# Attention and soft mixture of experts on one core: where v's factor is computed, when the next batch's inputs are loaded and split, and the order of the opening

## The chip, the core and the metric

The kernel runs on one core of one Trainium2 chip. The metric is the device time of one execution in microseconds (us). The core's engines run side by side and each works through its own list in order: TensorE (PE in the profile, with its weight loads as PEld) multiplies matrices into PSUM; VectorE (DVE) and ScalarE (ACT) do the element-wise work; GpSimd (POOL) does almost nothing here; SyncE (SP) issues the transfers (DMA) between HBM and the on-chip memory SBUF, also one after the other. An instruction that waits for another engine holds up everything behind it on its own list.

## The reference

```python
B, S, D, d_qk = 8, 2496, 256, 64
scores = (z @ z.T) / S                       # per batch, 2496 x 2496, symmetric
out    = u * (np.maximum(scores, 0) ** 2 @ v)
x      = out.reshape(8 * 2496, 256)
logits = x @ phi                             # 19968 x 32
d = softmax of logits over the tokens;  slots = d.T @ x
slot_out = relu(slots @ w1[e]) @ w2[e]       # 8 experts, 4 slots each
c = softmax of logits over the 32 slots;  result = c @ slot_out
```

The attention with relu and square takes most of the time: per batch, 2496 x 2496 scores and their product with v. Everything is single precision outside. Inside, z, the squared scores and v are each split into two half-precision parts (high and low), and three of the four products are summed. The half-precision parts need factors that bring the data into range: one per block of z, and one for v that depends on the largest bound over all of v in the batch.

## The kernel before, in words

**Tiling.** A batch has 5 blocks of 512 tokens (the last is padded to 448). For every block of queries (a *chunk*) the kernel runs through the 5 blocks of keys in two *halves* of 256 keys each, so a batch is 50 halves; with the last batch, whose last block is worked in two chunks of 256 queries, there are 410. The main loop `for h, x in enumerate(halves)` has one *step* per half. Step h puts the sums of half h on PE (`sums_halves` or `sums_whole`: 12 products of 128 rows and 512 columns, or 24 of 64 rows), and prepares a later half (`prepare(k)`, from step 18 on k = h + 3): PE computes the scores into the one PSUM tile `sc`, ACT applies relu and square into `r`, ACT or DVE rounds to half precision (`ph`), DVE subtracts to get the low part (`pl`). There are four buffers each of `r`, `ph` and `pl`, so at most some three halves can be ready ahead of PE.

**Symmetry.** A block pair that was computed once is not computed again: DVE transposes `r` (`y`), SP stores it to a scratch in HBM (`turned`), and later chunks fetch it back (`r<-turned`). Those halves are called turned: they need no scores, no relu and no square. In a batch's first chunk all ten halves are computed, in its last chunk (halves 40 to 49) eight of ten are turned. `lent` and `rd` are the same for the pair of a block with itself.

**Running sums.** A chunk's result gathers in a PSUM tile `acc`. There are two of these, used in turn; `next_acc()` takes the next one. When a chunk is finished, DVE multiplies it with u and `out_by` into `xg` (`finish_chunk`).

**The next batch's inputs.** While batch b-1 runs, z and v of batch b are brought in. The dictionary `splits` says at which step `load_z` or `load_v` is called (SP issues the load two steps before the number written there), and at which steps the functions that it returns run. These are, for z, `bound` (DVE, largest square) and `split` (ACT high part, DVE low part); for v, `squares` (ACT, tile `vq`, sum of squares into `energy`), `high` (ACT) and `low` (DVE). Raw data lands in 12 buffers with the tag `raw`, which z (5 tiles) and v (10 tiles) share: the eighth v load needs the buffer of the first z tile, and so on. The split parts go to 16 `blk` buffers for 15 tiles a batch.

**Factors.** `add_bounds` (a product with ones on PE) and `factors` (DVE) give z's. For v's, `largest` (DVE) leaves one number per partition in `few`; `scale_v(b, ps)` has PE spread these numbers over the PSUM tile `ps` in four small products, DVE reduces them back into `few` and computes `v_by` and `out_by`. `later` says at which steps these run. Before the change both `add_bounds` and `scale_v` take their PSUM tile with `next_acc()`, so that tile is afterwards the `acc` of the next chunk. `scale_v` is called at step 39 of the old batch, the last of its fourth chunk, and so uses the tile in which the fifth chunk's sums begin at step 40.

**Order.** Every PE, ACT, DVE and SP instruction goes through the class `InOrder` (line 74), which keeps the written order on each engine; that is why nearly all rows of the profile have the line L74, and tiles are the way to tell them apart. Small work is queued in the lists `middle`, `turning` and `behind` and run inside `prepare`: `behind` comes after the half's own work. `landing` and `later` feed `behind`.

**The token groups.** When 1024 tokens of x are complete, `groups(q)` adds fourteen small items to `work`, one per step. One of them computes the logits in the PSUM tile `ms`, of which there is one; the same tile also receives the slot sums of the group before. In the profile both have the name `lg`.

**Opening.** Before the loop, batch 0's z and v are loaded. z is bounded and scaled block by block (`first_z`, `add_bounds`, `factors`, `raise_z`), v's squares (`measure_v`), `largest` and `scale_v` follow, `keep_busy(n)` puts 2n products of ones on PE, and `prepare` is called for halves 0 to 3. One v tile is split before the loop and one in each step (`split_first_v`).

Of the kernel before, what the change touches and what calls it, by code (L numbers as in the profile page):

```python
# [8 lines left out]
F32 = mybir.dt.float32  # L9
# [4 lines left out]
AF = mybir.ActivationFunctionType  # L14
# [4 lines left out]
P = 128  # L19
# [6 lines left out]
QC = 512  # L26
# [5 lines left out]
NP = KT // 4  # L32
# [4 lines left out]
CATCH = 18  # L37
# [40 lines left out]
def attn_soft_moe_kernel(ctx, tc, uT, v, zz, phi, ww, outT):  # L78
    nc = tc.nc

    pe, act, dve, sp = (InOrder(tc, x) for x in (nc.tensor, nc.scalar, nc.vector, nc.sync))
# [73 lines left out]
    def add_bounds(b, ps, js):  # L155
        pe.matmul(
            ps[:, 0, js], nc.const_aps.tensor(1.0, [P, P], F32), tops[b % 2][:, js], start=True, stop=True
        )

    def factors(b, ps, js):  # L160


        n2, by = (t[b % 2][:, js] for t in (norm2, z_by))
        dve.tensor_scalar(bits(n2), bits(ps[:, 0, js]), EVEN, None, op0=ALU.bitwise_and)
        dve.tensor_scalar(
            bits(by), bits(n2), EVEN, 1, op0=ALU.bitwise_xor, op1=ALU.logical_shift_right
        )
        dve.tensor_scalar_mul(by, by, 2.0**77)
# [21 lines left out]
    def largest(b):  # L190


        root, w = v_by[b % 2], few[b % 2]
        n2 = norm2[b % 2].unsqueeze(2).to_broadcast([P, NP, 2])
        dve.tensor_scalar(
            bits(root), bits(energy[b % 2]), 1, ROOT, op0=ALU.logical_shift_right, op1=ALU.bitwise_and
        )
        r2 = root.rearrange("p (j i) -> p j i", i=2)
        dve.tensor_mul(r2, r2, n2)
        dve.reduce_max(w[:, 0:1], root, axis=AX.X)  # L200

    def scale_v(b, ps):


        w = few[b % 2]
        ps = ps[:, :, 2 * PAD :]
        for h, rows in enumerate(HALF):
            pe.matmul(
                ps[:, h], w[rows, 0:1].to_broadcast([64, P]), ident[rows, rows],
                start=True, stop=True,  # L210
            )
        dve.tensor_reduce(w[:, 2:4], ps, axis=AX.X, op=ALU.max)
        dve.scalar_tensor_tensor(w[:, 1:2], w[:, 2:3], 2.0**-120, w[:, 3:4], op0=ALU.max, op1=ALU.max)
        dve.tensor_scalar(
            bits(w[:, 2:3]), bits(w[:, 1:2]), EXPONENT, EXPONENT, op0=ALU.bitwise_and, op1=ALU.bitwise_xor
        )
        n2 = norm2[b % 2].unsqueeze(2).to_broadcast([P, NP, 2])
        dve.tensor_scalar(
            v_by[b % 2].rearrange("p (j i) -> p j i", i=2), n2, w[:, 2:3], 2.0**-51, op0=ALU.mult, op1=ALU.mult
        )  # L220
        dve.tensor_scalar(
            out_by[b % 2], norm2[b % 2], w[:, 1:2], 2.0**40 / S**2, op0=ALU.mult, op1=ALU.mult
        )
# [82 lines left out]
    halves = []  # L306
# [42 lines left out]
    def scores(k, ps=None, cut=slice(None)):  # L349


        x = halves[k]
        b, p = x.b, x.p
        j, o, n, t0 = x.ch
        if ps is None:
            ps = sc_ps.tile([P, 2, QC], F32, tag="sc", name=f"sc_{k}")
        m_all = QC if x.padded else n
        m = m_all // 2 if x.borrows else m_all

        def keys(t, c):  # L360
            return t[:, c * P : (c + 1) * P]

        i0 = 2 * x.borrows

        def queries(t):
            t = t.rearrange("k (i a q) -> k a i q", i=4, q=NS)
            return t[:, o // P : (o + m_all) // P, i0:][:, cut]

        def out(h):
            return ps[:, h, :m].rearrange("p (a i q) -> p a i q", i=4 - i0, q=NS)[:, cut]  # L370

        if k < RAW_SCORES:
            for h, rows in enumerate(HALF):
                pe.matmul(
                    out(h), keys(zraw[b, p][rows], 2 * x.w + h), queries(zraw[b, j][rows]),
                    start=True, stop=True,
                )
        else:
            zk, zq = zt[b, p], zt[b, j]
            for i, (kl, ql) in enumerate(((0, 0), (0, 1), (1, 0))):  # L380
                for h, rows in enumerate(HALF):
                    pe.matmul(
                        out(h), keys(zk[rows, kl], 2 * x.w + h), queries(zq[rows, ql]),
                        start=(i == 0), stop=(i == 2),
                    )
        return ps, m
# [3 lines left out]
    def high_low(k):  # L390

        if halves[k].ch[2] >= PAD + PAD:
            return [wa.tile([P, 2, QC], F16, tag=t, name=f"{t}_{k}", bufs=4) for t in ("ph", "pl")]
        i, j = divmod(k % 4, 2)
        if i not in quarters:
            quarters[i] = [
                wa.tile([P, 2, 2, QC // 2], F16, tag=t, name=f"{t}_{k}", bufs=4) for t in ("ph", "pl")
            ]
        return [t[:, j] for t in quarters[i]]

    def prepare(k):

# [451 lines left out]
    splits, later = {}, {}  # L854
    for b in range(1, B):
        base, order = (b - 1) * 2 * NP * NQ, BLOCKS[b == B - 1]
        z_at = [31, 32, 33, 39, 41]
        v_at = [47, 42, 43, 44, 45, 46, 48, 49, 50, 51]
        for i, (j, at) in enumerate(zip(order, z_at)):
            splits.setdefault(base + 11 + 2 * i, []).append((load_z, b, j, [base + 14 + 2 * i, base + at]))  # L860
        for i, at in enumerate(v_at):
            splits.setdefault(base + 27 + i, []).append(
                (load_v, b, i, [base + 27 + i, base + at, base + at])
            )
        later[base + 37] = lambda b=b: largest(b)
        later[base + 39] = lambda b=b: scale_v(b, next_acc())
        later[base + 25] = lambda b=b: add_bounds(b, next_acc(), slice(0, NP))
        later[base + 26] = lambda b=b: factors(b, accs[-1], slice(0, NP))
    landing, fetched = {}, set()
    accs = []  # L870

    def next_acc():

        accs.append(acc_ps.tile([P, 2, QC], F32, tag="acc", name=f"acc_{len(accs)}"))
        return accs[-1]
# [26 lines left out]
    def split_first_v():  # L902
        if v_splits:
            for f in v_splits.pop(0):
                f()
# [18 lines left out]
    def keep_busy(n):  # L924
        for _ in range(n):
            for h, rows in enumerate(HALF):
                pe.matmul(idle[:, h], ones[rows, 0:P], ones[rows], start=True, stop=True)
# [7 lines left out]
    def raise_z(p):  # L935
        dve.tensor_scalar_mul(zraw[0, p], zraw[0, p], z_by[0][:, p : p + 1])

    def measure_v(n):
        for _ in range(n):
            first_v.pop(0)()  # L940

    for js in (slice(0, 1), slice(1, 2), slice(2, NP)):
        for p in range(*js.indices(NP)):
            first_z[p]()
        add_bounds(0, idle, js)
        factors(0, idle, js)
        if js.start < 2:
            raise_z(js.start)
            keep_busy(2)
    prepare(0)  # L950
    measure_v(2)
    prepare(1)
    measure_v(8)
    keep_busy(8)
    for p in range(2, NP):
        raise_z(p)
    largest(0)
    scale_v(0, idle)
    prepare(2)
    split_first_v()  # L960
    prepare(3)
    acc = None
    for h, x in enumerate(halves):
        if x.begins:
            chunk = h // (2 * NP)
            acc = accs[chunk] if chunk < len(accs) else next_acc()
        last = len(halves) - h
        transfers(h)
        weights(last)
        if work and (x.at > 1 or last <= 20):  # L970
            work.pop(0)()
        behind.extend(landing.pop(h, ()))
        ahead = [k for k in range(h + 2 + (h > CATCH), h + 3 + (h >= CATCH)) if k < len(halves) and k >= 4]
        split_first_v()
        if not ahead and h < 2:
            run(middle)
            run(turning)
            run(behind)
            sums_halves(h, acc, 1, sums_halves(h, acc, 0, None))
        elif ahead and not halves[ahead[0]].turned:  # L980
            turn = sums_halves(h, acc, 0, None)
            prepare(ahead.pop(0))
            sums_halves(h, acc, 1, turn)
        else:
            if ahead and not x.ends:
                prepare(ahead.pop(0))
            elif not ahead:
                run(middle)
                run(behind)
                between_last(3 - last)  # L990
            sums_whole(h, acc)
        if x.ends:
            finish_chunk(x.b, x.ch, acc)
        for k in ahead:
            prepare(k)
        if h in FIRST_Z:
            z_splits.pop(FIRST_Z[h])()
        del pend[h]
# [300 lines left out]
```

## Time and profile before

| | us |
|---|---|
| median of 3 runs | 1387.83 (1386.79 to 1391.26) |
| the profiled execution's own time | 1392.14 |
| its span, first to last instruction | 1390.4 |
| PE busy in the span | 1283.8 |
| DVE busy | 1101.2 |
| ACT busy | 936.1 |
| one batch, about | 160 |
| first product with v on PE | at 31.66 |

PE's busy time counts a product at its modelled length, and products overlap, so 92% busy doesn't mean 92% of the peak. PE's clock is granted in steps, and a product takes twice as long at 0.50. The times of the table are of one execution; rows of a timeline carry the start, the length, the engine, the operation, output and inputs, and in brackets how long the engine stood idle before it and who released it.

### The profile page before, as it was taken

How to read it: one execution, taken by the hardware profiler on the slowest of the kernel's cores; microseconds unless marked ns; L12 is line 12 of the kernel's file. 1: busy time of each engine (PE TensorE's matmuls, PEld its weight loads, DVE VectorE, ACT ScalarE, POOL GpSimd, SP SyncE). 2: the span in 40 equal slices, each digit the busy share in tenths (PEclk: the TensorE clock that was granted, in tenths of full speed). 3: DMA queues.
4: the chain of work that ended last, by engine and by line, in shares of the span. 5: the costliest groups of instructions: out<-in, count | busy, mean ns of one | idle time of the engine just before them, and what ended most of it. 6: DMA issues, size and time to landing. Idle time of an engine off the chain costs nothing.

```text
span 1390.4 us, 27647 instructions
## 1 busy us (share of the span) xinstructions
PE 1283.8 (92%) x10969; PEld 617.5 (44%) x10969; DVE 1101.2 (79%) x1587; ACT 936.1 (67%) x1220; POOL 3.7 (0%) x22
## 2 busy tenths in 40 slices
PE   5999899998999799997999989998999989989984
PEld 2344355444544344443554444443554444434752
DVE  4788789777997779786998679877898679867663
ACT  5676788575966678575886658667886668754453
POOL 0000000000000000000000000000000000000000
PEclk7999999999999999999999999999999999999995
DMA  3577828784687737877387756878287766979959
GB/s 129 135 216 237 271 60 214 236 272 157 153 255 235 247 98 186 260 252 227 92 246 222 268 147 154 269 240 276 61 229 239 251 194 166 265 223 292 334 210 382
DMA packets 136402, 298.88 MB, mean 215 GB/s; under 512 B 17872, under 2 KB 38864, under 8 KB 124240
## 3 DMA queue, kind: packets, MB, share of 16 engines
q1 hardware_dynamic: 136272, 297.11, 69.9%
q8 instruction: 86, 1.41, 0.4%
q14 instruction: 44, 0.36, 0.1%
HBM read 162.04 MB, written 113.77 MB: 198 GB/s over the span
## 4 chain that ended last, share of the span: by engine, by line
PE 52%; DMA 14%; ACT 12%; DVE 9%; SPq 6%; issue 5%; DVEq 0%; ACTq 0%; POOLq 0%
PE acc L74 40%; PE sc L74 7%; SPq L74 6%; ACT r L74 6%; DMA r<-turned 4%; DMA vr<-in_v 4%; ACT ph L74 3%; DVE pl L74 3%; DVE y L74 2%; PE lg L74 2%; DMA turned<-y 2%; PE pf L74 1%; DMA w_own<-in_w 1%; ACT vq L74 1%; DMA xt<-y 1%
## 5 line engine op out<-in xcount | busy, mean ns | idle before, releaser
L74 PE MATMUL acc<-ph,v 64*128 64x512 f16 (+5 forms) x5036 | 944.5, 372 | 34.1 <-DVE few L74 30.1
L74 PEld LDWEIGHTS <-v 64*128 64x128 f16 (+1 forms) x7554 | 477.3, 96 | 569.3 <-issue 89.2
L74 PE MATMUL acc<-pl,v 64*128 64x512 f16 (+5 forms) x2518 | 608.7, 371 | 2.2 <-DVE pl L74 1.7
L74 DVE TENSOR_TENSOR pl<-r,ph 128x1024 f16<-128x1024 f32 (+1 forms) x410 | 467.3, 1146 | 166.2 <-ACT ph L74 154.7
L74 ACT CAST ph<-r 128x1024 f16<-128x1024 f32 (+1 forms) x286 | 288.3, 1017 | 149.2 <-PE acc L74 85.7
L74 ACT ACTIVATE r<-sc 128x1024 f32<-128x1024 f32 (+1 forms) x242 | 229.0, 946 | 144.7 <-PE sc L74 140.8
L74 ACT ACTIVATE r<-r 128x1024 f32<-128x1024 f32 (+1 forms) x242 | 238.4, 985 | 6.9
L74 DVE STREAM_TRANSPOSE y<-r 128x1024 f32<-128x1024 f32 x160 | 197.9, 1237 | 0.0
L74 PE MATMUL sc<-z,z 64*128 64x512 f16 x912 | 124.7, 377 | 7.6 <-ACT r L74 7.3
L74 PEld LDWEIGHTS <-z 64*128 64x128 f16 x1380 | 71.0, 94 | 90.0 <-issue 23.5
L74 ACT ACTIVATE vq<-vr 128x512 bf16<-128x512 f32 x80 | 49.8, 623 | 64.0 <-DMA vr<-in_v 63.7
L74 DVE CAST ph<-r 128x1024 f16<-128x1024 f32 (+1 forms) x124 | 74.1, 598 | 22.2 <-ACT r L74 21.8
L74 DVE SCALAR_TENSOR_TENSOR xg<-acc,out_by,ut 128x1024 f32<-128x1024 f32 (+7 forms) x57 | 51.5, 925 | 10.4 <-PE acc L74 10.4
L74 DVE SCALAR_TENSOR_TENSOR v<-vr,v_by,v 128x512 f16<-128x512 f32 x80 | 57.9, 724 | 0.0
L74 ACT ACTIVATE v<-vr,v_by 128x512 f16<-128x512 f32 x80 | 57.0, 715 | 0.0
L74 PE MATMUL sc<-z 64*128 64x512 f16 (+1 forms) x468 | 50.8, 321 | 5.1 <-ACT r L74 5.1
L74 DVE STREAM_TRANSPOSE y<-xg 128x512 f32<-128x512 f32 x72 | 49.4, 686 | 0.0
L74 DVE TENSOR_TENSOR pl<-rd,ph 128x512 f16<-128x512 f32 x36 | 23.9, 662 | 21.7 <-ACT ph L74 21.7
L74 DVE COPY ot<-pf 128x1024 f32<-128x1024 f32 (+1 forms) x20 | 24.0, 1198 | 21.0 <-PE pf L74 20.1
L74 ACT COPY ot<-pf 128x1024 f32<-128x1024 f32 (+1 forms) x20 | 19.8, 991 | 24.9 <-PE pf L74 20.7
L74 PE MATMUL lg<-xt 64*32 64x256 f32 x576 | 24.8, 402 | 12.1 <-DMA xt<-y 6.6
L74 ACT CAST ph<-rd 128x512 f16<-128x512 f32 x36 | 21.8, 605 | 11.6 <-DMA rd<-lent 11.6
(184 smaller groups left out, 540.7 us busy)
## 6 DMA issues: line engine op xcount, KB each, us to landing
turned<-y SPq DMA_DIRECT2D x320, 256.0 KB, 4.8
r<-turned SPq DMA_DIRECT2D x76, 1024.0 KB, 6.3
xt<-y SPq DMA_DIRECT2D x288, 72.0 KB, 3.1
vr<-in_v SPq DMA_DIRECT2D x80, 256.0 KB, 5.5
outT<-ot SPq DMA_DIRECT2D x18, 1024.0 KB, 6.9
ut<-in_uT SPq DMA_DIRECT2D x31, 512.0 KB, 5.6
lent<-yd SPq DMA_DIRECT2D x144, 64.0 KB, 2.9
rd<-lent SPq DMA_DIRECT2D x36, 256.0 KB, 3.7
```

What stands on the lines that cost most here:

```text
L74: return lambda *a, **k: self.tc.keep_in_program_order(f(*a, **k))
```

## The change

There are three edits.

1. **v's factor.** `scale_v(b, ...)` at step 39 takes an `ms` tile of its own instead of `next_acc()`. The fifth chunk's `acc` is then taken at step 40 by the loop. `largest` moves from step 37 to 36.
2. **Loads and splits of the next batch.** z's loads and bounds come two steps earlier. z's splits move from steps 31, 32, 33, 39, 41 to 27, 28, 29, 30, 39. v's load numbers go from 27 ... 36 to 23 ... 29 and 32, 33, 34, and `squares` runs one step after that number instead of at it: three steps after the load is issued instead of two, at steps 24 to 30 and 33 to 35. `add_bounds` and `factors` move from 25 and 26 to 23 and 24. The splits of v stay.
3. **Opening.** The new `prepare_first(k)` issues scores and relu and returns square, high and low as three functions. z's first block alone is measured and raised, half 0's scores and relu follow at once, then all ten squares of v on ACT; z's other blocks are measured after that. Half 0 is squared on DVE, not on ACT. `largest` and `scale_v` stand before the last steps of half 1, two v tiles are split before the loop, and half 3 is prepared inside the loop at step 1.

```diff
+    def prepare_first(k):
+        r = wa.tile([P, 2, QC], F32, tag="r", name=f"r_{k}", bufs=4)
+        pend[k] = hi, lo = high_low(k)
+        ps, _ = scores(k)
+        act.activation(r, ps, AF.Relu, scale=2.0**-22)
+        def square():
+            if k:
+                act.activation(r, r, AF.Square)
+            else:
+                dve.tensor_mul(r, r, r)
+        def high():
+            dve.tensor_copy(hi, r)
+        def low():
+            dve.tensor_sub(lo, r, hi)
+        return square, high, low
...
-        z_at = [31, 32, 33, 39, 41]
+        z_at = [27, 28, 29, 30, 39]
+        v_from = [23, 24, 25, 26, 27, 28, 29, 32, 33, 34]
         v_at = [47, 42, 43, 44, 45, 46, 48, 49, 50, 51]
         for i, (j, at) in enumerate(zip(order, z_at)):
-            splits.setdefault(base + 11 + 2 * i, []).append((load_z, b, j, [base + 14 + 2 * i, base + at]))
-        for i, at in enumerate(v_at):
-            splits.setdefault(base + 27 + i, []).append(
-                (load_v, b, i, [base + 27 + i, base + at, base + at])
+            splits.setdefault(base + 9 + 2 * i, []).append((load_z, b, j, [base + 12 + 2 * i, base + at]))
+        for i, (start, at) in enumerate(zip(v_from, v_at)):
+            splits.setdefault(base + start, []).append(
+                (load_v, b, i, [base + start + 1, base + at, base + at])
             )
-        later[base + 37] = lambda b=b: largest(b)
-        later[base + 39] = lambda b=b: scale_v(b, next_acc())
-        later[base + 25] = lambda b=b: add_bounds(b, next_acc(), slice(0, NP))
-        later[base + 26] = lambda b=b: factors(b, accs[-1], slice(0, NP))
+        later[base + 23] = lambda b=b: add_bounds(b, next_acc(), slice(0, NP))
+        later[base + 24] = lambda b=b: factors(b, accs[-1], slice(0, NP))
+        later[base + 36] = lambda b=b: largest(b)
+        later[base + 39] = lambda b=b: scale_v(b, ms_ps.tile([P, 2, 512], F32, tag="ms", name=f"mx_{b}"))
...
-    for js in (slice(0, 1), slice(1, 2), slice(2, NP)):
+    def measure_z(js):
         for p in range(*js.indices(NP)):
             first_z[p]()
         add_bounds(0, idle, js)
         factors(0, idle, js)
-        if js.start < 2:
-            raise_z(js.start)
-            keep_busy(2)
-    prepare(0)
-    measure_v(2)
-    prepare(1)
-    measure_v(8)
-    keep_busy(8)
+    measure_z(slice(0, 1))
+    raise_z(0)
+    keep_busy(1)
+    first = prepare_first(0)
+    measure_v(2 * NP)
+    measure_z(slice(1, 2))
+    raise_z(1)
+    for f in first:
+        f()
+    keep_busy(3)
+    measure_z(slice(2, NP))
+    keep_busy(3)
+    second = prepare_first(1)
+    second[0]()
+    keep_busy(3)
+    largest(0)
+    scale_v(0, idle)
+    second[1]()
+    split_first_v()
+    second[2]()
+    split_first_v()
     for p in range(2, NP):
         raise_z(p)
-    largest(0)
-    scale_v(0, idle)
     prepare(2)
-    split_first_v()
-    prepare(3)
...
-        ahead = [k for k in range(h + 2 + (h > CATCH), h + 3 + (h >= CATCH)) if k < len(halves) and k >= 4]
+        ahead = [k for k in range(h + 2 + (h > CATCH), h + 3 + (h >= CATCH)) if k < len(halves) and k >= 3]
         split_first_v()
-        if not ahead and h < 2:
+        if not ahead and h < 1:
```

## The prediction

> **What bounds the kernel now.** I read the page's first part, then who TensorE (PE) waits for, then the timeline around the longest of those waits.
>
> ```profile
> PE 1283.8 (92%) x10969; PEld 617.5 (44%) x10969; DVE 1101.2 (79%) x1587; ACT 936.1 (67%) x1220; POOL 3.7 (0%) x22
> ```
> ```profile
> PE acc L74 <- DVE few L74: 38.3, 14, 4.4
> ```
> PE has the least room, and its largest wait is for DVE's `few`: 14 waits, two at each of the seven changes of batch. The first of the seven, in the timeline of all engines:
>
> ```profile
> 161.27 1.23 DVE L74 TENSOR_TENSOR pl<-r,ph 128x1024 f16<-128x1024 f32 x1
> 161.38 0.44 PE L74 MATMUL acc<-ident,few 64*128 64x64 f32 x4 [0.35 <-DVE few L74]
> ...
> 163.94 1.21 DVE L74 TENSOR_TENSOR pl<-r,ph 128x1024 f16<-128x1024 f32 x1
> 165.06 0.74 DVE L74 SCALAR_TENSOR_TENSOR z<-zr,z_by,z 128x512 f16<-128x512 f32 x1
> 165.73 0.28 DVE L74 TENSOR_REDUCE few<-acc 128x2 f32<-128x128 f32 x1
> ...
> 166.06 0.91 PE L74 MATMUL acc<-ph,v 128*128 128x448 f16 x2 [4.25 <-DVE few L74]
> ...
> 166.70 1.22 DVE L74 TENSOR_TENSOR pl<-r,ph 128x1024 f16<-128x1024 f32 x1
> ```
> PE writes v's four small products into the next `acc` and cannot start half 40 in that tile until DVE has read them. DVE reads them only at 165.73, behind work for later halves, the old chunk's result and z's last split. The wait also costs clock. Windows, columns PE, PEld, DVE, ACT, POOL busy, then the granted clock: one inside the wait, then the 6 us after the first and the last of the seven restarts:
>
> ```profile
> 164.00:165.00 1.00, 0.00 (x0) 0.00 (x0) 1.00 (x2) 0.00 (x0) 0.00 (x0) 0.50 0.47 90
> ```
> ```profile
> 166.06:172.06 6.00, 6.00 (x20) 2.61 (x20) 2.40 (x6) 1.67 (x2) 0.00 (x0) 0.62 1.02 396
> ...
> 1126.93:1132.93 6.00, 6.00 (x25) 2.80 (x25) 3.03 (x7) 1.73 (x3) 0.00 (x0) 0.76 0.65 206
> ```
> At 0.50 a product takes twice its time, so what is lost is (1 - clock) x 6 us. With the seven clocks 0.62, 0.76, 0.61, 0.60, 0.69, 0.76, 0.76 that is 2.28 + 1.44 + 2.34 + 2.40 + 1.86 + 1.44 + 1.44 = 13.2 us. Waits and clock together are 38.3 + 13.2 = 51.5 us, or 7.36 us per change of batch.
>
> **Edit 1, v's factor.** With `ms` as the target, half 40 no longer waits for DVE's reduction. The four products (0.44 us) and DVE's five small operations stay. The work order decides whether PE then merely waits for the next thing. A half of this chunk takes PE 2.27 us, by the chain of waits:
>
> ```profile
> 185.65 2.27 PE acc L74 x24
> ```
> From 161.82 it needs the low parts `pl` of halves 40, 41, 42, 43 at 161.8, 164.1, 166.3 and 168.6. By the timeline the `pl` that starts at 161.27 is half 41's (ready 162.5), that of 163.94 half 42's (165.15), that of 166.70 half 43's (167.92). All are in time, the last by 0.7 us.
>
> Later DVE has to keep up: PE's chunk shrinks by 7.36 us and DVE's work doesn't. Windows from the wait to the moment at which half 49 is ready, and over the new batch's first chunk, and the two rows of half 49:
>
> ```profile
> 161.82:189.25 27.43, 23.19 (x194) 11.47 (x196) 20.42 (x36) 12.01 (x19) 0.00 (x0) 0.88 0.35 122
> ...
> 194.81:227.00 32.19, 31.87 (x298) 16.70 (x296) 31.14 (x38) 29.74 (x34) 0.00 (x0) 1.00 0.72 173
> ```
> ```profile
> 188.56 0.69 DVE L74 TENSOR_TENSOR pl<-r,ph 128x512 f16<-128x512 f32 x1
> ...
> 192.46 0.54 PE L74 MATMUL acc<-ph,v 64*128 64x448 f16 x4
> ```
> Half 49 is ready at 189.25, 3.2 us before PE takes it. Afterwards PE takes it at 192.46 - 7.36 = 185.1, and DVE, without any gap, has it at 161.82 + 20.42 - 0.74 (z's low part, moved ahead by edit 2) = 181.5. DVE can't be quite gapless, since each rounding waits for a buffer that PE frees, so the lead shrinks by up to some 1.5 us, and in the first chunk DVE is busy 31.14 of 32.19 us and can't rebuild it. I take all 1.5 as lost: 7.36 - 1.5 = 5.86 us per change, **41.0 us** for seven. Bounds: 51.5 (nothing lost), and 23.5 (the first rival below).
>
> Does the clock's share come back too? It does if no long wait remains. [...]
>
> **Edit 2, loads and splits.** ACT waits for v's raw data, and SP is held by z's late splits, because the eighth to tenth v load reuses z's buffers:
>
> ```profile
> ACT vq L74 <- DMA vr<-in_v: 63.7, 21, 6.3
> ```
> ```profile
> SPq L74 <- DVE z L74: 28.4, 15, 3.9
> ```
> ```profile
> vr<-in_v SPq DMA_DIRECT2D x80, 256.0 KB, 5.5
> ```
> ```profile
> 200.82 2.59 PE acc L74 x24
> 204.06 2.59 PE acc L74 x24
> ```
> A load lands 5.5 us after issue, and the square stands two steps behind it. PE's sums of a half take 2.59 us, with scores between them the pitch is 204.06 - 200.82 = 3.24. Two steps are 2 x 2.59 = 5.2 us, too short. Three steps are 7.8 us. Three of ten squares per batch wait now. What it costs PE shows in the windows ahead of two of the changes, where ACT catches up:
>
> ```profile
> 300.00:312.00 12.00, 10.72 (x101) 5.18 (x99) 8.93 (x11) 11.87 (x21) 0.00 (x0) 1.00 0.76 253
> 786.00:798.00 12.00, 9.61 (x86) 4.56 (x83) 9.71 (x14) 11.84 (x21) 0.00 (x0) 1.00 0.66 236
> ```
> PE lacks 1.28 us in the first and 2.39 us in the second, 1.84 on average. Against it: squares now also stand at steps 24 and 25, where ACT prepares direct halves with relu, square and cast:
>
> ```profile
> L74 ACT CAST ph<-r 128x1024 f16<-128x1024 f32 (+1 forms) x286 | 288.3, 1017 | 149.2 <-PE acc L74 85.7
> L74 ACT ACTIVATE r<-sc 128x1024 f32<-128x1024 f32 (+1 forms) x242 | 229.0, 946 | 144.7 <-PE sc L74 140.8
> L74 ACT ACTIVATE r<-r 128x1024 f32<-128x1024 f32 (+1 forms) x242 | 238.4, 985 | 6.9
> ...
> L74 ACT ACTIVATE vq<-vr 128x512 bf16<-128x512 f32 x80 | 49.8, 623 | 64.0 <-DMA vr<-in_v 63.7
> ```
> ```profile
> 159.97 0.72 ACT L74 ACTIVATE z<-zr,z_by 128x512 f16<-128x512 f32 x1
> ```
> That is 0.95 + 0.99 + 1.02 + 0.62 + 0.19 (the read of the sum behind each square, as in the opening's row at 24.31) = 3.77 us of ACT against PE's pitch of 3.24 us: 0.5 us behind in two steps, 1.1 us per batch, covered by the halves prepared ahead; without that cover 7 x 1.1 = 7.7 us lost. The z splits in steps 28 to 30 fall on turned halves, where ACT has 1.02 + 0.72 + 0.81 = 2.55 us in PE's 2.59. The z loads two steps earlier and `add_bounds` at 23 only need data and an `acc` that are ready by then; I cost them at nothing, under PE's sums. I take half of what PE lacks, 0.9 x 7 = **6.3 us**; bounds -7.7 and 1.83 x 7 = 12.8.
>
> **Edit 3, opening.** Rows of the timeline:
>
> ```profile
> 5.52 0.49 DVE L74 TENSOR_SCALAR cw<-cw,z_by 128x512 f32<-128x512 f32 x1
> ...
> 11.00 2.08 PE L74 MATMUL sc<-cw 64*128 64x512 f32 x4
> ...
> 13.13 1.02 ACT L74 ACTIVATE r<-sc 128x1024 f32<-128x1024 f32 x1 [10.90 <-PE sc L74]
> ...
> 24.31 0.19 ACT L74 ACTIVATION_READ_ACCUMULATOR vq<-vr 128x1 f32 x1
> ...
> 26.69 0.22 DVE L74 TENSOR_SCALAR v_by<-norm,few 128x10 f32<-128x10 f32 x1
> ...
> 27.79 1.02 ACT L74 ACTIVATE r<-sc 128x1024 f32<-128x1024 f32 x1 [3.30 <-PE sc L74]
> ...
> 31.66 0.61 PE L74 MATMUL acc<-ph,v 64*128 64x512 f16 x2 [0.71 <-ACT v L74]
> ```
> Block 0 of z is raised at 6.0 in both. After the change its scores follow at once (to 8.3) and relu (to 9.4), then ten squares at 0.62 + 0.19 less overlap, 0.75 us each: to 17.0, if v has landed by then. DVE has the other z blocks and half 0's square, cast and low part (some 3.1 us at 1.2, 0.7, 1.2): to about 15.5. Then PE: ones (I put 1.0, half of the scores' time), half 1's scores (2.08), ones again (1.0), the factor's products (0.44): 20.0. `v_by` then comes at about 21, not 26.9. v's first split is now ahead of half 2's preparation, so PE's first sums start after half 2's scores, at 22 to 23 instead of 31.66, about 9 us earlier. Half 3 is prepared only inside the loop and takes back 1 to 2 us. I take **7.5 us**. Upper bound: ACT starts 13.13 - 8.3 = 4.8 us earlier, loses its pause of 3.3 us between 24.5 and 27.8 and one square (0.99): 9.1. Lower: the 4.8 less a pause of 1.6 until half 1's scores: 3.
>
> **Sum.** 41.0 + 6.3 + 7.5 = 54.8 us off the profiled execution's own 1392.14 (its span of 1390.4 and 1.7 around it) gives 1337.3. That execution lies 4.3 us above the median, 1387.83, so the median should come to **1333**. With all lower bounds (23.5 - 7.7 + 3 = 18.8) it is 1369, with all upper ones (51.5 + 12.8 + 9.1 = 73.4) 1314.
>
> **Rivals.**
> *DVE takes PE's place.* If no lead is left when the new batch begins, its first six steps, in which v's splits go on, run at DVE's pace. By the low parts' starts of 194.75 and 198.44 a half takes 3.7 us there, and I put DVE's need at 3.9 at most, PE's is 3.24: 6 x 0.66 = 4.0 us per change given back, 3.36 x 7 = 23.5 us stay, and the median is 1387.8 - 23.5 - 6.3 - 7.5 = 1350. For it: DVE's 31.14 of 32.19. Against: half 49's 3.2 us of lead.
>
> ```profile
> 194.75 1.23 DVE L74 TENSOR_TENSOR pl<-r,ph 128x1024 f16<-128x1024 f32 x1
> ...
> 198.44 1.23 DVE L74 TENSOR_TENSOR pl<-r,ph 128x1024 f16<-128x1024 f32 x1 [0.35 <-ACT ph L74]
> ```
> *The wait moves to the logits.* `ms` has one buffer, and in four of the seven changes the logits come right behind half 41:
>
> ```profile
> 173.01 1.89 PE lg L74 x64
> ...
> 972.56 1.89 PE lg L74 x64
> ```
> These are the first and the last of the four. PE would get there at 161.82 + 2 x 2.27 = 166.4, DVE's reduction ends at 166.01: 0.4 us in hand. If DVE is late by more, those four changes keep their wait and their clock: 4 x 5.86 = 23.4 us, median 1356.
> *No gain.* DVE and ACT set the pace everywhere and PE's waits only move: 1388. Against: the rows behind the restarts, where DVE is busy 2.40 and 3.03 us of 6 and so not at its limit.
> *Slower.* The squares now stand among the fetches of turned halves. If SP issues a load more than 7.8 - 5.5 = 2.3 us late, its square waits again, and ACT's list is in order: relu and casts of the next halves stand behind it. With all ten squares of a batch waiting the present mean of 63.7 / 21 = 3.0 us, ACT loses 30 us per batch instead of 9.1. The cover is three halves, 7.8 us; the rest, 30 - 9.1 - 7.8 = 13 us, falls on PE: 7 x 13 = 92 us lost against 41.0 + 7.5 gained, 1431. It decides from about eight waiting squares a batch on ((48.5 / 7 + 9.1 + 7.8) / 3.0). Against: only three of ten wait with two steps.
>
> **How the numbers follow.** Forecast (1316 to 1345) 0.58; DVE in PE's place 0.18; logits 0.11; still faster than 1316, 0.03; no gain 0.04; slower 0.06. A difference under 0.3%, 4 us, can't be told from none. Faster: 0.58 + 0.18 + 0.11 + 0.03 = 0.90, same 0.04, slower 0.06. The range of 1314 to 1369 holds the forecast and the first two rivals, 0.87, and both sums of the bounds.
>
> **What would show it.** Edit 1: no wait of PE for `few` above 1 us, clock 1.00 around the changes of batch, DVE near 0.9 behind them. Edit 2: fewer than seven waits of ACT for `vr` in all, and PE without gaps in the 20 us ahead of a change. Edit 3: the first `acc` product at 22 to 23, and half 3's some 8 us earlier than before. The forecast is wrong if a new wait of over 2 us stands at the changes (for `pl`: the first rival; for `lg`: the second), or if ACT's waits for `vr` grow (the last).

## The result, and the profile after

The median fell from 1389.55 to 1308.85 us (1306.67 to 1309.35; the kernel before ran beside it, 1386.79 to 1394.17). The ratio is 0.9413, with a 95% interval of 0.9383 to 0.9443: 80.7 us off. The forecast was 1333 in a range of 1314 to 1369. The direction was right and the size too small, by more than all upper bounds together allowed (73.4 us). The profiled execution took 1308.94 us, its span is 1307.1.

The first part of the page of the kernel after with the shares of its chain, and the chain's shares before:

```profile
PE 1257.1 (96%) x10965; PEld 608.6 (47%) x10965; DVE 1100.1 (84%) x1588; ACT 934.2 (71%) x1219; POOL 3.7 (0%) x22
...
PE 74%; DMA 9%; ACT 8%; DVE 4%; SPq 3%; issue 2%; ACTq 0%; DVEq 0%; POOLq 0%
```
```profile
PE 52%; DMA 14%; ACT 12%; DVE 9%; SPq 6%; issue 5%; DVEq 0%; ACTq 0%; POOLq 0%
```

DVE's and ACT's busy times are those of before. PE's fell by 26.7 us with the same products but for four of ones: 7.0 us of it in the opening and 15.9 in the six batches between the changes, where the mean clock rose from 0.98 to 1.00 (windows below). Its idle time within the span fell from 1390.4 - 1283.8 = 106.6 to 1307.1 - 1257.1 = 50.0. PE's share of the chain that ended last rose from 52% to 74%.

Where the 83.3 us of span went is read from four windows of each trace. They end at half 4's scores in the opening, at the first and at the seventh of v's small products (one set at each change of batch), and at the end of the span. The columns are the window, its length, PE, PEld, DVE, ACT and POOL busy, the clock, and the DMA share and rate. Before:

```profile
0.00:41.90 41.90, 26.75 (x122) 9.63 (x124) 20.27 (x46) 20.09 (x35) 2.93 (x20) 0.80 0.39 124
41.90:161.38 119.48, 116.19 (x891) 50.91 (x887) 96.14 (x121) 93.16 (x117) 0.00 (x0) 1.00 0.72 215
...
161.38:1122.25 960.87, 908.67 (x7657) 430.27 (x7657) 799.89 (x1153) 675.92 (x870) 0.00 (x0) 0.98 0.70 207
...
1122.25:1390.40 268.15, 232.21 (x2303) 126.64 (x2303) 184.94 (x269) 146.91 (x200) 0.79 (x2) 0.91 0.77 258
```

After:

```profile
0.00:28.62 28.62, 19.75 (x118) 8.42 (x120) 18.55 (x45) 19.55 (x35) 2.93 (x20) 0.82 0.45 157
28.62:144.83 116.21, 114.93 (x891) 51.65 (x887) 99.03 (x124) 92.86 (x118) 0.00 (x0) 1.00 0.77 228
...
144.83:1046.18 901.35, 892.81 (x7657) 423.60 (x7656) 797.96 (x1153) 674.56 (x870) 0.00 (x0) 1.00 0.74 220
...
1046.18:1307.10 260.92, 229.64 (x2304) 124.96 (x2303) 184.57 (x269) 147.27 (x199) 0.79 (x2) 0.92 0.80 265
```

The opening gave 13.3 us, the rest of batch 0 3.3, the six batches between the changes 59.5 and the last change with its tail 7.2. In the six batches PE's busy time fell by 908.67 - 892.81 = 15.9 us and its idle time from 52.2 to 8.5, so by 43.7. The waits of PE between the first and the last change say which idle time. Before, and then after (total us, times, longest):

```profile
PE acc L74 <- DVE few L74: 33.7, 12, 4.4
PE sc L74 <- ACT r L74: 10.8, 22, 1.7
```
```profile
PE lg L74 <- DMA xt<-y: 5.8, 7, 2.2
PE sc L74 <- ACT r L74: 1.7, 6, 0.3
```

The wait for `few` is gone as a wait of PE, and the wait of the scores for ACT's `r` has shrunk by 9.1 us. The two make 42.8 of the 43.7. The first of them was in the forecast as a row; the second was not looked at as a term of its own.

At the first change of batch, the timeline after shows:

```profile
144.83 0.44 PE L74 MATMUL mx<-ident,few 64*128 64x64 f32 x4
...
149.34 0.28 DVE L74 TENSOR_REDUCE few<-mx 128x2 f32<-128x128 f32 x1
...
149.84 1.09 PE L74 MATMUL lg<-xg,phi_sb 64*32 64x256 f32 x32
```

DVE's reduction is as far behind the small products as before (4.5 us, before 161.38 to 165.73 = 4.35), but PE has sums to work on. It reaches the logits 0.2 us after the reduction ends. Behind this change the clock is full, and DVE close to its limit:

```profile
150.00:156.00 6.00, 6.00 (x87) 3.25 (x76) 5.83 (x15) 3.27 (x7) 0.00 (x0) 1.00 1.03 397
```

On ACT and SP, the waits that edit 2 was about, after:

```profile
ACT vq L74 <- DMA vr<-in_v: 11.6, 9, 2.5
```
```profile
SPq L74 <- DVE z L74: 1.7, 3, 0.8
```

The squares' wait fell from 63.7 to 11.6 us, SP's wait for z's splits from 28.4 to 1.7.

### The profile page after: what moved, and what is told of

The parts are those of the page before. It is cut to its first block, busy times and chain, and to the rows that moved or that the text cites. A ratio compares the mean times of both kernels' runs of the same rounds, so it can differ in the third digit from the quotient of the medians.

```text
span 1307.1 us, 27632 instructions
## 1 busy us (share of the span) xinstructions
PE 1257.1 (96%) x10965; PEld 608.6 (47%) x10965; DVE 1100.1 (84%) x1588; ACT 934.2 (71%) x1219; POOL 3.7 (0%) x22
## 4 chain that ended last, share of the span: by engine, by line
PE 74%; DMA 9%; ACT 8%; DVE 4%; SPq 3%; issue 2%; ACTq 0%; DVEq 0%; POOLq 0%
PE acc L74 59%; PE sc L74 9%; ACT r L74 4%; SPq L74 3%; PE lg L74 3%; DMA xt<-y 2%; DMA r<-turned 1%; DVE pl L74 1%; DMA w_own<-in_w 1%; ACT ph L74 1%; DMA outT<-ot 1%; PE pf L74 1%; DMA turned<-y 1%; DVE y L74 1%; ACT v L74 1%
## 5 line engine op out<-in xcount | busy, mean ns | idle before, releaser
L74 PE MATMUL acc<-ph,v 64*128 64x512 f16 (+5 forms) x5036 | 930.9, 369 | 1.7 <-DVE ph L74 0.6
L74 PEld LDWEIGHTS <-v 64*128 64x128 f16 (+1 forms) x7554 | 470.3, 95 | 525.5 <-issue 40.2
L74 PE MATMUL acc<-pl,v 64*128 64x512 f16 (+5 forms) x2518 | 602.3, 369 | 1.5 <-DVE pl L74 1.2
L74 DVE CAST ph<-r 128x1024 f16<-128x1024 f32 (+1 forms) x124 | 74.1, 598 | 10.5 <-ACT r L74 10.2
L74 ACT ACTIVATE vq<-vr 128x512 bf16<-128x512 f32 x80 | 49.8, 623 | 11.8 <-DMA vr<-in_v 11.6
L74 PE MATMUL lg<-xt 64*32 64x256 f32 x576 | 24.7, 405 | 11.6 <-DMA xt<-y 6.2
L74 DVE TENSOR_TENSOR pl<-rd,ph 128x512 f16<-128x512 f32 x36 | 23.9, 664 | 11.8 <-ACT ph L74 11.8
```

Of the source, the lines that this page charges most:

```text
L74: return lambda *a, **k: self.tc.keep_in_program_order(f(*a, **k))
```

## The experiments

Each kernel ran in three rounds beside the kernel before (medians of before 1390.26, 1390.34 and 1392.0 us in the three groups). The ratios can be compared with each other and with the 0.9413 of the whole change.

| | median us | ratio to before (95%) |
|---|---|---|
| edit 1 alone | 1347.31 | 0.9679 (0.9646 to 0.9712) |
| edit 2 alone | 1369.78 | 0.9847 (0.9820 to 0.9873) |
| edit 3 alone | 1378.14 | 0.9907 (0.9876 to 0.9938) |
| edits 2 and 3 | 1353.24 | 0.9727 (0.9703 to 0.9751) |
| after, squares two steps behind the issue | 1308.46 | 0.9424 (0.9403 to 0.9446) |
| after, z's splits late again | 1308.05 | 0.9413 (0.9386 to 0.9441) |
| after, all of z late again | 1308.06 | 0.9403 (0.9374 to 0.9432) |
| after, `largest` at step 37 | 1308.39 | 0.9422 (0.9398 to 0.9446) |
| after, v's loads and squares late again | 1326.80 | 0.9541 (0.9499 to 0.9583) |
| after, opening without ones | 1305.88 | 0.9404 (0.9373 to 0.9435) |
| after, one more low part at each change | 1313.51 | 0.9443 (0.9410 to 0.9475) |
| after, three more | 1340.16 | 0.9638 (0.9598 to 0.9678) |

### Which edit gives how much

**Edit 1 alone**, on the kernel before:

```diff
-        later[base + 39] = lambda b=b: scale_v(b, next_acc())
+        later[base + 39] = lambda b=b: scale_v(b, ms_ps.tile([P, 2, 512], F32, tag="ms", name=f"mx_{b}"))
```

> The kernel before with edit 1 alone: v's factor in the logits' tile; largest, loads, splits and opening as before. Theory A (the whole loss of waits and clock at the seven changes of batch comes back, with no help from the other edits): 51.5 us off, about 1338 where before is 1389.5, and no wait of PE for few above 1 us. Theory B (the prediction: DVE's lead shrinks): 41 us off, about 1348. Theory C (DVE has no lead without the earlier loads, and PE waits for pl or for largest instead): 30 us or less off, 1360 or more, with PE still waiting 1 to 3 us for few ahead of the small products.

It took 43.0 us off (1390.26 - 1347.31). PE's waits in the whole run:

```profile
PE mx L74 <- DVE few L74: 7.9, 7, 1.7
```

The second wait of each change is gone. The first is still there under another tile's name: the small products themselves wait for `few`, which `largest` leaves late. So this edit could never have had the whole row of 38.3 us. Its own share is 38.3 - 7.9 = 30.4 us of waits and 13.2 of clock, 43.6 together, and it got nearly all of that.

**Edit 2 alone** is the loop's dictionary of after with `scale_v` in `next_acc()`:

```diff
-        z_at = [31, 32, 33, 39, 41]
+        z_at = [27, 28, 29, 30, 39]
+        v_from = [23, 24, 25, 26, 27, 28, 29, 32, 33, 34]
...
-                (load_v, b, i, [base + 27 + i, base + at, base + at])
+                (load_v, b, i, [base + start + 1, base + at, base + at])
```

> The kernel before with edit 2 alone: loads, bounds, squares, z's splits, add_bounds and largest at the new steps; v's factor still in the next acc, opening as before. Theory A (edit 2 saves PE about 2.6 us per batch by itself): 18 us off, about 1371. Theory B (the prediction's size, 0.9 us per batch): 6 us off, 1383. Theory C (the long wait at the change lets DVE and ACT catch up, so that earlier loads are worth little while it stands): 0 to 4 us off, 1386 to 1390, though ACT's waits for vr fall from 63.7 to about 12 us.

It took 20.5 us off, three times the forecast's 6.3. PE's waits in the whole run:

```profile
PE acc L74 <- DVE few L74: 32.7, 7, 4.9
...
PE sc L74 <- ACT r L74: 4.8, 10, 1.1
```

Seven waits for `few` are left of fourteen. The first of each pair has gone with this edit, and 9.9 us of the scores' waits for `r` with it (14.7 before).

**Edit 3 alone** is the kernel after with the loop's dictionary of before. **Edits 2 and 3** are the kernel after with one line back:

```diff
-        later[base + 39] = lambda b=b: scale_v(b, ms_ps.tile([P, 2, 512], F32, tag="ms", name=f"mx_{b}"))
+        later[base + 39] = lambda b=b: scale_v(b, next_acc())
```

> The kernel after with the whole block of later steps (edits 1 and 2) put back as before, so edit 3 alone. Theory A (read from the two traces, where the scores of half 4 start at 28.62 instead of 41.90): 13.3 us off, 1376. Theory B (the prediction): 7.5 us off, 1382. Nothing in the batches behind should change: the seven waits for few stay at 38 us.

> The kernel after with v's factor back in the next acc: edits 2 and 3. If the edits add up, the time is that of before less what e2 and e3 save; against the kernel after it is longer by what e1 saves: 1309 + 51.5 = 1360 (theory A) or 1309 + 41 = 1350 (theory B). If edit 2 only helps together with edit 1, it is 1374 to 1376, the opening's gain alone.

Edit 3 alone took 12.1 us off, edits 2 and 3 together 37.0. The three edits alone add up to 43.0 + 20.5 + 12.1 = 75.6 us, and together they gave 80.7. The intervals of the single ratios are some 4 us wide to each side, so a joint gain of 5 us is not shown. On top of the other two, edit 1 is worth (0.9727 - 0.9413) x 1390 = 44 us.

### What in edit 2 gives it

Three kernels undo one part each, on the kernel after.

```diff
-                (load_v, b, i, [base + start + 1, base + at, base + at])
+                (load_v, b, i, [base + start, base + at, base + at])
```

> The kernel after with v's squares at the step number of the load instead of one behind it: two steps between issue and square, the rest as in after (near 1309, 1390 before). Theory A (edit 2's gain comes from the third step, which covers the landing of 5.6 us): ACT's waits for vr return from 12 to 40 us or more, PE's waits for relu in sc return to some 10 us, 1317 to 1325. Theory B (the gain comes from freeing SP and from z's splits out of the crowded steps): waits for vr stay under 25 us, 1309 to 1313.

```diff
-        z_at = [27, 28, 29, 30, 39]
+        z_at = [31, 32, 33, 39, 41]
```

> The kernel after with z's splits back at steps 31, 32, 33, 39 and 41, so that the eighth to tenth v loads wait on SP for z's buffers again, and everything behind them on SP. Theory B: SP's waits for z return to 28 us or more, the last three squares of a batch wait, largest comes late and PE waits for few again: 1317 to 1330. Theory A (the third step is what counts, seven of ten loads don't depend on z): 1309 to 1314.

```diff
-        later[base + 36] = lambda b=b: largest(b)
+        later[base + 37] = lambda b=b: largest(b)
```

> The kernel after with largest back at step 37, nothing else. In e1_factor_only, with largest at 37 and late squares, PE still waited 7.9 us for few ahead of the small products. Theory A (that wait was ACT and DVE running late for want of v's data): no wait returns, 1307 to 1311. Theory B (it is largest's place behind half 40's low part): about 8 us of waits for few return, 1315 to 1319.

None of the three costs anything that these runs can tell. Yet the first two did bring waits back: the first kernel ACT's for `vr`, to a size between its two expectations, and the second one SP's for z's splits, though without the waits of PE for `few` that were expected behind it:

```profile
ACT vq L74 <- DMA vr<-in_v: 26.6, 14, 3.8
```
```profile
SPq L74 <- DVE z L74: 38.6, 17, 7.0
```

14 squares wait and SP stands for 38.6 us, with no loss of time. So neither the third step, nor SP's wait for z's splits, nor the step of `largest` is what edit 2 gains by. Two more kernels separate z from v. In one all of z goes back, in the other v's loads and squares go back to the steps of before:

```diff
-        z_at = [27, 28, 29, 30, 39]
+        z_at = [31, 32, 33, 39, 41]
...
-            splits.setdefault(base + 9 + 2 * i, []).append((load_z, b, j, [base + 12 + 2 * i, base + at]))
+            splits.setdefault(base + 11 + 2 * i, []).append((load_z, b, j, [base + 14 + 2 * i, base + at]))
...
-        later[base + 23] = lambda b=b: add_bounds(b, next_acc(), slice(0, NP))
+        later[base + 25] = lambda b=b: add_bounds(b, next_acc(), slice(0, NP))
```

(`factors` goes back from 24 to 26 likewise.)

> The kernel after with all of z back at the old steps: loads, bounds, add_bounds at 25, factors at 26, splits at 31, 32, 33, 39, 41; v as after. Theory A (v's place counts): 1306 to 1312, as e8_z_late was. Theory B (z's place counts): 1320 to 1330.

```diff
-        v_from = [23, 24, 25, 26, 27, 28, 29, 32, 33, 34]
+        v_from = [27, 28, 29, 30, 31, 32, 33, 34, 35, 36]
...
-                (load_v, b, i, [base + start + 1, base + at, base + at])
+                (load_v, b, i, [base + start, base + at, base + at])
...
-        later[base + 36] = lambda b=b: largest(b)
+        later[base + 37] = lambda b=b: largest(b)
```

> The kernel after with v's loads, squares and largest at the old steps (loads numbered 27 to 36, squares at the same number, largest 37); z's loads and splits, v's factor and the opening stay as after (near 1309, 1390 before). Theory A (edit 2's gain comes from v's loads standing four steps earlier in SP's list, ahead of the stores and fetches that hold it): nearly all of what e2_loads_only saved is lost, 1324 to 1332, with ACT's waits for vr at 40 us or more and PE waiting for few ahead of the small products again. Theory B (z's earlier loads and splits are what counts): 1309 to 1314.

All of z is worth nothing that these runs can tell; v's place is worth (0.9541 - 0.9413) x 1390 = 18 us, nearly all of edit 2. With v late, ACT and PE wait as in the kernel before:

```profile
ACT vq L74 <- DMA vr<-in_v: 52.7, 28, 4.8
```
```profile
PE sc L74 <- ACT r L74: 13.0, 27, 1.6
...
PE mx L74 <- DVE few L74: 4.7, 7, 1.1
```

PE's gaps return in the place where edit 2 had closed them. These are the busy times in the 20 us ahead of v's small products, summed over the seven changes: before, with edit 2 alone, and with v late.

```profile
sum 140.00, PE 121.58 PEld 55.39 DVE 113.04 ACT 130.94 POOL 0.00; mean PE 17.37 PEld 7.91 DVE 16.15 ACT 18.71 POOL 0.00
```
```profile
sum 140.00, PE 140.00 PEld 61.36 DVE 101.19 ACT 112.99 POOL 0.00; mean PE 20.00 PEld 8.77 DVE 14.46 ACT 16.14 POOL 0.00
```
```profile
sum 140.00, PE 123.60 PEld 57.26 DVE 105.88 ACT 127.50 POOL 0.00; mean PE 17.66 PEld 8.18 DVE 15.13 ACT 18.21 POOL 0.00
```

PE lacks 18.4 us before, nothing with edit 2 alone (nor in the kernel after), and 16.4 us with v late.

The landing of a load has not changed: the median is 5.5 us before, 5.6 after and 5.8 in this run. What changed is when SP gets to issue it. Before, in a stretch of batch 1: SP's wait between 270 and 288, two rows of its list, and the square on ACT that waited:

```profile
SPq L74 <- DVE y L74: 6.0, 1, 6.0
```
```profile
276.53 2.87 SPq L74 DMA_DIRECT2D turned<-y  x4
...
287.72 1.38 SPq L74 DMA_DIRECT2D vr<-in_v  x1
```
```profile
295.81 0.63 ACT L74 ACTIVATE vq<-vr 128x512 bf16<-128x512 f32 x1 [4.19 <-DMA vr<-in_v]
```

SP stands for 6.0 us until DVE has transposed the half that `turned<-y` stores, and v's loads stand behind that store and the next ones. The one that gets out at 287.72 lands 8 us later, and ACT waits 4.2 us for it. SP's waits for such transposes add up to much the same before and after (217.9 and 203.0 us); it is v's loads that have moved among them. In the same batch after, the first load is out at 232.40 and its square stands 21 us later, without a wait:

```profile
232.40 0.99 SPq L74 DMA_DIRECT2D vr<-in_v  x1
```
```profile
253.23 0.62 ACT L74 ACTIVATE vq<-vr 128x512 bf16<-128x512 f32 x1
```

The kernel with v late moves loads, squares and `largest` together, so it does not say how much of the 18 us the squares' own steps on ACT's list account for. That the loads' place in SP's list is what counts is read from the waits; no run separates the two.

### The opening

```diff
     raise_z(0)
-    keep_busy(1)
...
         f()
-    keep_busy(3)
     measure_z(slice(2, NP))
-    keep_busy(3)
     second = prepare_first(1)
     second[0]()
-    keep_busy(3)
```

> The kernel after without the ten pairs of products of ones behind the first block's factors (the six pairs at the very start stay). Theory A (the part of the opening that was underestimated is PE's clock: the ones keep it at full speed until the first sums): the first sums and half 1's scores run at clock 0.5 for some 4 us, 3 to 6 us longer, 1312 to 1315. Theory B (the order alone makes the opening's gain): same or up to 2 us shorter, as PE has 3 us less to do, 1306 to 1309.

The products of ones do nothing for the time that these runs can tell. Without them the clock was at half speed for ten microseconds and back soon after the first sums, which start at 19.33 (windows of this kernel):

```profile
10.00:20.00 10.00, 5.82 (x18) 2.20 (x20) 7.04 (x22) 8.95 (x21) 0.00 (x0) 0.50 0.49 177
20.00:30.00 10.00, 9.88 (x80) 4.21 (x82) 8.94 (x12) 7.80 (x10) 0.00 (x0) 0.96 0.01 2
```

Its median, 1305.88, is the lowest of all, but its interval overlaps that of the kernel after, so it is no better as far as these runs can tell. In the traces the scores of half 4 start at 27.76 without the ones and at 28.62 with them. Nor did the ones hold the clock: in the kernel after it is 0.50 from 15 to 17 us. What the opening gains comes from the order of the work, not from PE being kept busy.

### How much room is left

Half 42's low part is computed again on DVE, right behind the small products at the seven changes, once or three times more. The repeated work changes no value.

```diff
                 dve.tensor_sub(lc[:, h, :, cols], src[:, h], hc[:, h, :, cols])
+                if k < 350 and k % 50 == 42:
+                    for _ in range(1):
+                        dve.tensor_sub(lc[:, h, :, cols], src[:, h], hc[:, h, :, cols])
```

> The kernel after with one more low part on DVE at each change of batch: half 42's is computed twice, 1.22 us more of DVE ahead of what PE needs next, seven times. Theory A (DVE's lead behind the change is not used up): 0 to 2 us longer, 1309 to 1311. Theory B (the prediction's: the lead is down to about 1.8 us and can't be rebuilt in the first chunk): up to 7 x 1.2 = 8.5 us longer where the lead is gone, some 4 us on average, 1313.

> The same with three more low parts, 3.7 us of DVE per change. Theory A: PE loses only what exceeds its lead of 3 to 4 us, 0 to 5 us in all, 1309 to 1314. Theory B: 7 x (3.7 - 1.8) = 13 us or more, 1322 to 1335. If DVE were the bound all along, 7 x 3.7 = 26 us, 1335.

One more (1.2 us of DVE) costs (0.9443 - 0.9413) x 1390 = 4 us by the ratios, whose intervals overlap; PE then waits 4.5 us for `few` ahead of the four sets of logits. The 1313.5 us meet the 1313 of Theory B, but the wait is not the one that it names. Three more (some 3.7 us) cost (0.9638 - 0.9413) x 1390 = 31 us, 4.5 at each change, and 1340 lies above all that was expected. PE's waits, and the first change, in that run:

```profile
PE lg L74 <- DVE few L74: 14.6, 4, 3.7
...
PE acc L74 <- DVE pl L74: 9.6, 6, 2.7
```
```profile
154.26 1.96 PE L74 MATMUL lg<-xg,phi_sb 64*32 64x256 f32 x32 [3.55 <-DVE few L74]
```
```profile
150.00:156.00 6.00, 2.45 (x40) 1.10 (x46) 5.83 (x10) 1.77 (x2) 0.00 (x0) 0.81 1.01 397
```

The second rival's wait is there, at the four changes where the logits follow, and with it the lost clock: the same 32 products take 1.96 us instead of 1.09. PE's busy time rises by 1268.9 - 1257.1 = 11.8 us in this run with the same 10965 products, while the mean clock of the execution falls from 0.979 to 0.969; this had not been counted in what was expected. The rest, at `pl`, is DVE setting the pace. Both rivals stand within about a microsecond of the kernel after.

## Why the prediction was right or wrong

**Edit 1: the size nearly right (41.0 forecast, 43.0 alone, 44 on top of the others), by two errors that cancel, which is luck.** The first was to book the whole row of 38.3 us on this edit. The row held two waits per change. The second, for the reduction, belongs to the tile. The first, 7.9 us in seven, is PE waiting for `largest`, and it is late because v's squares are late. It stays with edit 1 alone and goes with edit 2 alone, so 43.6 us were there to be had and not 51.5. The second error was the loss of 1.5 us of lead at each change, 10.5 in all: of the 43.6 us, 43.0 came. That pair of rows, half 49's low part and PE's product, reads after:

```profile
165.46 0.69 DVE L74 TENSOR_TENSOR pl<-r,ph 128x512 f16<-128x512 f32 x1
...
169.36 0.54 PE L74 MATMUL acc<-ph,v 64*128 64x448 f16 x4
```

From 165.46 + 0.69 = 166.15 to 169.36 are 3.2 us, as before. But these rows can't tell how much lead DVE has. They stand as far apart in the run with three added low parts, at the third change, where PE had stood 2.69 us for `pl` at 462.69 because DVE was late:

```profile
476.53 0.69 DVE L74 TENSOR_TENSOR pl<-r,ph 128x512 f16<-128x512 f32 x1
...
480.43 0.54 PE L74 MATMUL acc<-ph,v 64*128 64x448 f16 x4
```

DVE comes to this half after a pause for ACT (1.51 us before, 0.87 after, 0.46 here), and ACT after one for PE's scores, which start 3.4 us ahead of the low part in all three kernels. So PE itself sets the distance. The margins that decide are the smaller ones right behind the small products, 0.7 us for half 43's low part and 0.4 us for the logits by the forecast's own reckoning.

In the old kernel ACT and DVE had stood still behind the restart until PE freed buffers (waits from 166.1 to 189, ACT's and DVE's):

```profile
ACT ph L74 <- PE acc L74: 9.9, 3, 8.5
```
```profile
DVE pl L74 <- ACT ph L74: 5.0, 2, 3.5
```

That slack is what paid for the faster PE: DVE is now busy 5.83 us of the six that follow the change, not 2.40. The share of the clock, by contrast, came back as reckoned: 13.2 us forecast, and with edit 1 alone PE's busy time fell from 1283.8 to 1270.7 us, by 13.1.

**Edit 2: the term that failed (6.3 forecast, bound 12.8, measured 20.5).** Two steps went wrong. The price was read from windows of 12 us that ended before the change, and half of it was taken. The windows that follow them, up to the small products, were left out. This is the one behind the first of them:

```profile
312.00:319.97 7.97, 6.11 (x32) 2.49 (x28) 6.12 (x15) 6.13 (x9) 0.00 (x0) 1.00 0.97 309
```

PE lacks another 7.97 - 6.11 = 1.86 us there, so 3.14 with the 1.28 of the first window. Over all seven changes it lacks 18.4 us in the last 20 (the sums above), which is nearly all of the 20.5 that edit 2 alone gave.

The mechanism was also wrong. The argument set two steps (5.2 us) and three (7.8) against a landing of 5.5 us. But with the loads early in SP's list, squares two steps behind them cost nothing that the runs can tell (0.9424 against 0.9413 with three), and the late loads of batch 1 were issued behind stores that had held SP (6.0 us at one of them), not at their step. The half that was taken off for late squares in crowded steps of ACT was not needed. The bound of -7.7 us, ACT falling behind in steps 24 and 25, did not show: ACT's waits fell.

**Edit 3: too small (7.5 forecast, bound 9.1, measured 12.1 alone and 13.3 between the traces).** The rows of the opening after:

```profile
5.86 1.13 PE L74 MATMUL sc<-cw 64*128 64x512 f32 x4 [0.51 <-DVE cw L74]
...
19.17 0.22 DVE L74 TENSOR_SCALAR v_by<-norm,few 128x10 f32<-128x10 f32 x1
...
20.42 0.39 PE L74 MATMUL acc<-ph,v 64*128 64x512 f16 x2 [0.57 <-ACT v L74]
```

The first sums start at 20.42, 11.2 us earlier than before, not 9. Half 0's scores took 1.13 us, not 2.08, and `v_by` came at 19.17 rather than 21. The second part is that nothing was given back at half 3. From the first sums to half 4's scores, before and then after:

```profile
31.66:41.90 10.24, 9.32 (x60) 3.31 (x62) 7.31 (x9) 3.75 (x5) 0.00 (x0) 0.71 0.33 71
```
```profile
20.42:28.62 8.20, 7.69 (x64) 3.32 (x66) 7.56 (x12) 7.14 (x9) 0.00 (x0) 1.00 0.01 2
```

The old kernel's first sums ran at a clock of 0.71, which the forecast had not read from its own trace. The stretch is 10.24 - 8.20 = 2.0 us shorter, in place of 1 to 2 lost.

**The rivals.** DVE took no place of PE's (waits for `pl` 1.2 us in the whole run), the wait did not move to the logits, and ACT did not fall behind. The margin of 0.4 us that the forecast gave the logits was about right: PE arrives 0.2 us after the reduction, and the added low parts show what lies behind it. The rival of late squares was far off, since it let each square wait for a landing that now is past by then.

**What was to be seen.** No wait for `few` over 1 us, clock 1.00 at the changes, DVE near its limit behind them, PE without gaps ahead of them: all four hold at all seven changes (the clock is 1.00 in the 20 us on either side of the small products, and DVE is busy 18.8 to 19.1 of the 20 behind them). Nine waits for `vr` miss the "fewer than seven", though they are short. The first sums came 1.6 us earlier than 22.

**The sum.** The three edits measured alone exceed their forecasts by 2.0, 14.2 and 4.6 us, 20.8 of the 25.9 that the forecast missed. The other 5 us are the difference between the three edits together and their sum, which the intervals do not separate from nothing.

## What to carry to other kernels

A row of waits adds up what may have several causes: before it is booked on one edit, look at each of its members in the timeline, since the first and the second wait at one place can belong to different parts of a change. A lead is to be read where nothing that the bottleneck itself does sets the time. When an engine's lateness is priced, the window must reach to the point where the work is in step again, and a load's lead is to be counted from the moment at which its queue can issue it, behind the stores that wait ahead of it (6.0 us for one of them here), not from the step at which it is written. Slack that looks used up on a busy engine may only be its waiting for the engine that is to become faster.

## What the runs showed of the hardware

In the two waits that were read, of 4.25 and 3.55 us, the clock fell before the wait was over. In the kernel before, PE was idle from 161.82 on; the windows from 163 to 164 and from 164 to 165 us have the clock at 0.91 and 0.50, so it fell 2.0 us after PE stopped. Cut at 163.8, 164, 170.5 and 170.7, the stretch from 161 to 172 reads 1.00 or 0.50 everywhere but in the two short windows in which the clock changed (0.54 and 0.64). In the run with three added low parts PE was idle from 150.71 to 154.26, and the window from 150 to 156 us reads 0.81. Taken as 1.00 and then 0.50, that is 12 x 0.19 = 2.3 us at half speed, so the clock fell at about 153.7, some 3.0 us after PE stopped.

The way back is read from the clocks of the first 6 us behind the seven restarts before (0.60 to 0.76): 12 x (1 - clock) us were at half speed, 2.9 to 4.8 and 3.8 on average. The opening without ones took longer: PE had products from 13.74 on, with one pause of 0.43 us before 17.46, and they reached their full-speed length only at about 20.8, 7 us later (clock 0.50 in each window of 1 us from 17 to 20, 0.61 from 20 to 21).

```profile
17.46 2.08 PE L74 MATMUL sc<-cw 64*128 64x512 f32 x4 [0.43 <-ACT r L74]
...
20.78 0.60 PE L74 MATMUL acc<-ph,v 64*128 64x512 f16 x4
```

The clock column itself was not to be trusted in the old opening. It reads 1.00 here, while the four products of half 0's scores at 11.00 took 2.08 us, nearly twice the 1.13 of the kernel after:

```profile
10.00:20.00 10.00, 6.85 (x26) 2.52 (x26) 4.18 (x9) 6.72 (x12) 0.00 (x0) 1.00 0.51 183
```

Why it does is open; the lengths of the products are the safer reading there.
